# Transposed inverse-Fourier matrices issued during the convolution, and parameter rows loaded from ScalarE's queue into buffers of their own

## The chip, the cores and the metric

The kernel runs on one core of a Trainium2 chip. The metric is the device time of one execution in microseconds (us), from a launch to its end; the profile adds the span from the first to the last instruction. The core has five engines with an instruction stream each: TensorE (PE, matrix products), VectorE (DVE), ScalarE (ACT), GpSimd (POOL) and SyncE (SP). SP, ACT and POOL also issue the DMAs. An engine works through its stream in order, so an instruction that waits holds all that stand behind it on that engine. PE writes its products into banks of PSUM, which ACT or DVE must empty.

## The reference

The kernel computes a block's output and all its gradients, with 2048 tokens, 576 channels, 4608 hidden channels and 128 state pairs per channel:

```
xn = layernorm(x)
K[d,l] = Re( sum_n C[d,n] * exp(dt_d * A[d,n] * l) * dt_d * B[d,n] )
s  = causal convolution of xn with K (by FFT) + xn * Dskip
g  = silu( (silu(xn @ w1) * (xn @ w3)) @ w2 )
out_0 = x + s * g
out_1 ... out_12 = gradients of x, A_re, A_im, B_re, B_im, C_re, C_im, log_dt, Dskip, w1, w3, w2 for grad_out
```

out_2 and out_3 are the gradients of A_re and A_im, out_4 to out_7 those of B and C, out_10 to out_12 those of w1, w3 and w2.

## The kernel before, in words

A scheduler orders the instructions of each engine from planned times (`self.at`), from dependencies and from explicit `issue_after` marks. The stages, with their times in the profiled execution:

- To about 480 us: layer norm, the hidden products and the kernel K, and the forward convolution by matrix products with the Fourier matrices dC and dS (`conv_half`, `dft_block`, L868). The hidden activations are stored to H_dram (L1139).
- `ffn_output` (L1145), to about 690 us: 16 token tiles. For each, SP transposes one tile of H_dram into one of three buffers hcA, hcB, hcC (`begin`, through `nat_transpose`, L1775), and PE multiplies it with w2 (`product`, L1216) into po. SP also stores the tile's results (GS_dram L1237, out_0 L1244) and loads parts of the backward stage (w2T, w2r).
- `backward` (L1614): 18 groups of 256 hidden channels. In each, PE forms ph (L1852) and the weight gradients in pgw (L1893, L1913, L1925); ACT copies them out of PSUM (CAST, L1855, L1897, L1915, L1928); DVE multiplies; SP stores GU and GG (L1875). pgw has two banks. Between the groups stand the backward convolution, in four quarters, and from its end the parameter sums: 36 chunks in two halves, for which SP loads qT (L1775), gz (L1477) and pz (L1480), PE forms et_ps (L1491), and DVE multiplies and sums into S_all (L1496, L1499, through the single buffer pr_q).
- `phase6_inputs`, from about 1435 us: 16 token tiles again. SP transposes GG and GU of a tile into one of two buffers acts (L1775), PE multiplies them with w1 and w3 (px, L1964), DVE adds (gx, L2012), and `ln_bwd_tile` follows: ACT (L2031), POOL (sc, L2039 and L2040), ACT (gxs, L2041), POOL (gxs, L2042), DVE (go, L2071), POOL's store (L2073). ACT loads gxs and go for it (L1953, L1955).

Two pieces are touched by the change. `dft_turn_kernel` fills idC and idS, the matrices of the inverse transform in the backward convolution, by eight transposes of D_dram on SP. The two tiles take the place of dC and dS. Each of the eight is marked to be issued after one of the hc loads of tiles 5 to 12. `phase5_blocks` finishes the parameter gradients in five blocks (four of 2 x 64 rows and one of 2 x 32): twelve loads of rows of B, C and A into X_b on POOL (L1556), the sums ST on DVE (L1561), products with X_b (L1568), a transpose on PE (L1575) that ACT scales back into ST (L1577), products (L1581), eight stores of out_4 to out_7 on POOL (L1587), products (L1591), a copy into X_b on ACT (L1595), and four stores of out_2 and out_3 from it on POOL (L1598). X_b, ST and WO_b share the three buffers of the tag gh6. Each `yield` gives the turn back to the stage around it, which calls the next piece after certain steps of the chunks.

DMAs that SP and ACT issue tell of their landing through eight semaphores, DMAHW0 to DMAHW7, which they take by turns, both engines from the same eight; POOL's DMAs have eight of their own, DMASW0 to DMASW7. In the built program a DMA waits for the semaphore's last DMA where nothing else has made sure of it.

Of the kernel before, what the change touches and what calls it, by code (L numbers as in the profile page):

```python
# [14 lines left out]
BF16 = mybir.dt.bfloat16  # L15
I32 = mybir.dt.int32
I16 = mybir.dt.int16
P = 128
# [82 lines left out]
class K:  # L101
# [745 lines left out]
    def dft_turn_kernel(self):  # L847
        mats = []
        for m, tag in enumerate(("dC", "dS")):
            t = self.matp.tile([P, 4, self.cfg.LS], BF16, name="i" + tag, tag=tag)  # L850
            for i in range(4):
                with self.tc.issue_after(self.hc_loads[5 + 4 * m + i].ins):
                    self.nc.sync.dma_start_transpose(out=t[:, :, i * P:(i + 1) * P], in_=self.D_dram[m, i])
            mats.append(t)
        self.dC, self.dS = mats

# [448 lines left out]
    def params_open(self, S_all, ps):  # L1305
        cfg = self.cfg
        self.sums = ExitStack()
        gkp = self.sums.enter_context(self.pool(name="g_k", bufs=1, side="right"))
        self.qp = self.sums.enter_context(self.pool(name="g_q", bufs=2, side="right"))
        self.zp = self.sums.enter_context(self.pool(name="g_z", bufs=3, side="right"))  # L1310
        self.prp = self.sums.enter_context(self.pool(name="g_pr", bufs=1, side="right"))
        self.S_all, self.ps_T = S_all, ps
        self.gz = []
        for i in range(3):
            z = gkp.tile([P, 2, 2, 2, 8, cfg.LT], BF16, name=f"gz{i}")
            self.nc.vector.memset(z[:], 0.0)
            self.gz.append(z)
        self.half = 0
        self.loaded = {}
# [164 lines left out]
    def param_half(self, ch, dg, gK, qT, pz):  # L1484
# [8 lines left out]
        for x in range(2):  # L1493
# [5 lines left out]
            nc.vector.tensor_reduce(out=self.S_all[:, :, d0:d0 + 4],  # L1499
                                    in_=pr[:].rearrange("p r k (d a) -> p (r k) d a", d=4), op=ALU.add, axis=AX.X)  # L1500

# [39 lines left out]
    def phase5_blocks(self):  # L1541
        nc, cfg, aps = self.nc, self.cfg, self.aps
        D, N = cfg.D, cfg.N
        H = D // 2
        fp = self.fp
        names = ("A_B_re", "A_B_im", "A_C_re", "A_C_im", "A_A_re", "A_A_im")
        tt = nc.vector.tensor_tensor
        for j, c0 in enumerate(range(0, H, 64)):
            R = min(64, H - c0)
            v = slice(0, 2 * R)  # L1550
            if j:
                yield 0
            X = fp.tile([P, 6, N], BF16, name="X_b", tag="gh6")
            for k, name in enumerate(names):
                for h in range(2):
                    nc.gpsimd.dma_start(out=X[R * h:R * h + R, k, :], in_=aps[name][H * h + c0:H * h + c0 + R, :])  # L1556
            yield (c0 + R) // 8
            sv = self.S_all[:].rearrange("p r (c h) -> p r h c", h=2)[:, :, :, c0:c0 + R]
            ST = fp.tile([P, 4, N], FP32, name="ST", tag="gh6")
            sm = ST[:, :, 0:2 * R].rearrange("p k (h c) -> p k h c", h=2)  # L1560
            tt(out=sm[:, 0:2], in0=sv[:, 0:4:2], in1=sv[:, 5:8:2], op=ALU.subtract)  # L1561
            tt(out=sm[:, 2:4], in0=sv[:, 1:4:2], in1=sv[:, 4:8:2], op=ALU.add)
            WO = fp.tile([P, 4, N], FP32, name="WO_b", tag="gh6")
            W = WO[:, 0:2]
            O = WO[:, 2:4].bitcast(BF16).rearrange("p k (two n) -> p (k two) n", two=2)
            Q = self.prp.tile([P, 2, 4, N], FP32, name="pr_q")
            for k in range(2):
                tt(out=Q[v, k, 0:2], in0=X[v, 2 + k:3 + k].to_broadcast([2 * R, 2, N]), in1=X[v, 0:2], op=ALU.mult)  # L1568
            tt(out=W[v, 0], in0=Q[v, 0, 0], in1=Q[v, 1, 1], op=ALU.subtract)
            tt(out=W[v, 1], in0=Q[v, 0, 1], in1=Q[v, 1, 0], op=ALU.add)  # L1570
            yield 0
            pt = self.ps_T.tile([P, 4, N], FP32, name="et_ps")
            with self.tc.issue_after(self.pe_last.ins):
                for k in range(4):
                    nc.tensor.transpose(pt[v, k, :], ST[:, k, 0:2 * R], self.ident_f[:])  # L1575
            for k in range(2):
                nc.scalar.activation(out=ST[v, k:4:2], in_=pt[v, k:4:2], func=ACT.Copy, scale=self.dtb[v, k, j:j + 1])  # L1577
            yield 0
            Q = self.prp.tile([P, 2, 4, N], FP32, name="pr_q")
            for k in range(2):  # L1580
                tt(out=Q[v, k], in0=ST[v, 2 * k:2 * k + 1].to_broadcast([2 * R, 4, N]), in1=X[v, 0:4], op=ALU.mult)  # L1581
            tt(out=O[v, 0:2], in0=Q[v, 0, 0:4:2], in1=Q[v, 1, 1:4:2], op=ALU.subtract)
            nc.vector.scalar_tensor_tensor(out=O[v, 2:4], in0=Q[v, 0, 1:4:2], scalar=-1.0, in1=Q[v, 1, 0:4:2],
                                           op0=ALU.mult, op1=ALU.subtract)
            for k, on in enumerate(("out_6", "out_4", "out_7", "out_5")):
                for h in range(2):
                    nc.gpsimd.dma_start(out=aps[on][H * h + c0:H * h + c0 + R, :], in_=O[R * h:R * h + R, k])  # L1587
            yield 0
            Q = self.prp.tile([P, 2, 4, N], FP32, name="pr_q")
            for k in range(2):  # L1590
                tt(out=Q[v, k, 0:2], in0=W[v, k:k + 1].to_broadcast([2 * R, 2, N]), in1=ST[v, 1:4:2], op=ALU.mult)  # L1591
            tt(out=ST[v, 1], in0=Q[v, 0, 0], in1=Q[v, 1, 1], op=ALU.subtract)
            nc.vector.scalar_tensor_tensor(out=ST[v, 3], in0=Q[v, 0, 1], scalar=-1.0, in1=Q[v, 1, 0],
                                           op0=ALU.mult, op1=ALU.subtract)
            nc.scalar.copy(out=X[v, 0:2], in_=ST[v, 1:4:2])  # L1595
            for k, on in enumerate(("out_2", "out_3")):
                for h in range(2):
                    nc.gpsimd.dma_start(out=aps[on][H * h + c0:H * h + c0 + R, :], in_=X[R * h:R * h + R, k])  # L1598
            acc = self.acc
            for k, (a, b) in enumerate(((ST[v, 1:4:2], X[v, 4:6]), (ST[v, 0:1], W[v, 0:1]), (ST[v, 2:3], W[v, 1:2]))):  # L1600
                nc.vector.tensor_tensor_reduce(out=Q[v, 1, 2:4] if k == 0 else Q[v, 1, 2:3], in0=a, in1=b, scale=1.0, scalar=0.0,
                                               op0=ALU.mult, op1=ALU.add, accum_out=acc[v, k:k + 1])
            tt(out=acc[v, 0:1], in0=acc[v, 0:1], in1=acc[v, 1:2], op=ALU.add)
            tt(out=self.gl[v, j:j + 1], in0=acc[v, 0:1], in1=acc[v, 2:3], op=ALU.subtract)
        yield 0
        pt = self.ps_T.tile([P, 512], FP32, name="et_ps")
        with self.tc.issue_after(self.pe_last.ins):
            nc.tensor.transpose(pt[0:self.NB, 0:P], self.gl, self.ident_f[:])
        gr = fp.tile([self.NB, P], BF16, name="lg_b", tag="gh6")
        nc.scalar.copy(out=gr[:], in_=pt[0:self.NB, 0:P])  # L1610
        for row, vec in self.block_rows(gr, aps["out_8"]):
            nc.gpsimd.dma_start(out=vec, in_=row)
# [567 lines left out]
```

## Time and profile before

| | |
|---|---|
| median of 3 executions | 1776.63 us (1776.33 to 1779.44) |
| the profiled execution | 1770.22 us, span 1768.4 us |
| mean granted clock of PE | 0.983 |
| idle time of PE before its longest waits | 8.33 us at 676, 7.03 us at 717, 5.22 us at 1714 |
| POOL's DMA issues in `phase5_blocks` | about 0.5 us each |
| ACT's DMA issues in the last stage | about 0.34 us each |

In a list of instructions each row has the start and the duration in us, the engine (SPq and ACTq are the queues that issue DMAs), the line, the operation, out<-in with sizes, a count, and in brackets the idle time before it and what ended it. In the table of windows the columns are the stretch, its length, the busy time of PE, PEld, DVE, ACT and POOL with counts, the granted clock of PE, the mean busy share of the DMA engines, and GB/s. The list of DMA issues gives out<-in, queue, count, size and the median time from issue to landing, where known.

### The profile page before, as it was taken

How to read it: one execution, taken by the hardware profiler on the slowest of the kernel's cores; microseconds unless marked ns; L12 is line 12 of the kernel's file. 1: busy time of each engine (PE TensorE's matmuls, PEld its weight loads, DVE VectorE, ACT ScalarE, POOL GpSimd, SP SyncE). 2: the span in 40 equal slices, each digit the busy share in tenths (PEclk: the TensorE clock that was granted, in tenths of full speed). 3: DMA queues.
4: the chain of work that ended last, by engine and by line, in shares of the span. 5: the costliest groups of instructions: out<-in, count | busy, mean ns of one | idle time of the engine just before them, and what ended most of it. 6: DMA issues, size and time to landing. Idle time of an engine off the chain costs nothing. (4 is left out here: it accounts for less than half of the span.)

```text
span 1768.4 us, 34842 instructions
## 1 busy us (share of the span) xinstructions
PE 1632.5 (92%) x13765; PEld 1196.9 (68%) x13765; DVE 1360.9 (77%) x2221; ACT 894.1 (51%) x1509; POOL 328.5 (19%) x530
## 2 busy tenths in 40 slices
PE   6889999999999997799999999999999998999987
PEld 2444444454547775688888888888788776778866
DVE  7658889879784653777978889659899965877765
ACT  4878888886862113565756666554445411110001
POOL 3101111112142110011111101111111233141132
PEclk9999999999999998999999999999999999999999
DMA  7879999978799996768675857589998999999981
GB/s 206 274 252 363 340 352 357 366 251 262 247 279 261 229 219 149 209 183 230 190 193 168 217 171 210 162 233 247 244 244 226 213 260 215 227 242 214 240 172 47
DMA packets 633771, 414.03 MB, mean 234 GB/s; under 512 B 427479, under 2 KB 578247, under 8 KB 628999
## 3 DMA queue, kind: packets, MB, share of 16 engines
q1 hardware_dynamic: 586780, 285.38, 65.2%
q0 software_dynamic: 32704, 114.32, 20.1%
q10 hardware_dynamic: 14122, 12.10, 2.4%
q8 instruction: 108, 1.77, 0.4%
q14 instruction: 57, 0.46, 0.1%
HBM read 130.88 MB, written 191.94 MB: 183 GB/s over the span
## 5 line engine op out<-in xcount | busy, mean ns | idle before, releaser
L1120 PE MATMUL pgu<-wmB_w,xnT 128*128 128x512 bf16 x1152 | 277.1, 379 | 2.5 <-ACT gu_t L1133 2.4
L1964 PEld LDWEIGHTS <-acts 128*128 128x128 bf16 x2304 | 227.9, 100 | 66.1 <-DMA acts<-GU_dram 3.5
L1913 PEld LDWEIGHTS <-xn_bf 128*128 128x128 bf16 x2304 | 224.1, 98 | 42.2 <-issue 16.2
L1496 DVE TENSOR_TENSOR pr_q<-et_ps,pz 128x1024 f32<-128x1024 f32 x144 | 175.9, 1221 | 34.2 <-PE et_ps L1491 25.9
L1964 PE MATMUL px<-wT,acts 128*128 128x288 bf16 x1472 | 193.7, 290 | 0.0
L1120 PEld LDWEIGHTS <-xnT 128*128 128x128 bf16 x1152 | 106.9, 98 | 120.3 <-issue 21.3
L1499 DVE TENSOR_REDUCE S_all<-pr_q 128x32 f32<-128x1024 f32 x144 | 175.2, 1217 | 3.2
L1852 PE MATMUL ph<-w2T,goT 128*128 128x256 bf16 x1440 | 172.8, 274 | 4.6 <-ACT gh L1855 4.6
L1852 PEld LDWEIGHTS <-goT 128*128 128x128 bf16 x1440 | 139.9, 98 | 23.6 <-issue 7.2
L1893 PE MATMUL pgw<-go_o,h_n 128*128 128x288 bf16 x1152 | 148.8, 286 | 0.2
L1133 ACT CAST gu_t<-pgu 128x1024 bf16<-128x1024 f32 x144 | 147.5, 1024 | 0.0
L1913 PE MATMUL pgw<-gu_n,xn_bf 128*128 128x256 bf16 x1152 | 134.5, 272 | 9.2 <-ACT gw L1897 5.3
L1913 PE MATMUL pgw<-gg_n,xn_bf 128*128 128x256 bf16 x1152 | 130.4, 272 | 2.1 <-ACT gw L1915 2.0
L1893 PEld LDWEIGHTS <-h_n 128*128 128x128 bf16 x1152 | 112.1, 98 | 29.5 <-issue 1.8
L1132 ACT ACTIVATE s_t<-pgu 128x512 bf16<-128x512 f32 x144 | 87.9, 610 | 85.2 <-PE pgu L1120 44.3
L1141 POOL DMA_DIRECT2D GUF_dram<-gu_t x72 | 65.3, 908 | 339.2 <-ACT gu_t L1133 312.9
L1915 ACT CAST gw<-pgw 128x256 bf16<-128x256 f32 x144 | 52.2, 373 | 143.2 <-PE pgw L1913 143.2
L1964 PE MATMUL px<-wA,acts 128*128 128x288 bf16 x832 | 113.5, 294 | 5.2 <-DMA acts<-GU_dram 2.9
L1855 ACT CAST gh<-ph 128x512 bf16<-128x512 f32 x144 | 81.6, 601 | 59.1 <-PE ph L1852 57.1
L2031 ACT ACTIVATE go<-gx 128x576 bf16<-128x576 f32 x15 | 10.3, 683 | 186.0 <-DVE gx L2012 179.4
L1136 DVE TENSOR_TENSOR h_t<-s_t,gu_t 128x1024 bf16<-128x1024 bf16 x72 | 49.4, 687 | 47.7 <-ACT gu_t L1133 46.7
L1898 POOL DMA_DIRECT2D out_dram<-gw x36 | 20.2, 560 | 341.7 <-ACT gw L1897 237.7
(329 smaller groups left out, 3016.9 us busy)
## 6 DMA issues: line engine op xcount, KB each, us to landing
GUF_dram<-gu_t POOLq DMA_DIRECT2D x72, 512.0 KB, 5.9
H_dram<-h_t SPq DMA_DIRECT2D x72, 256.0 KB, 5.4
Q_dram<-q_k SPq DMA_DIRECT2D x36, 512.0 KB, 3.9
gg_n<-GUF_dram POOLq DMA_DIRECT2D x18, 1024.0 KB, 6.5
h_n<-GUF_dram POOLq DMA_DIRECT2D x18, 1024.0 KB, 8.8
GG_dram<-gg_n SPq DMA_DIRECT2D x36, 512.0 KB, 10.6
GU_dram<-gu_n SPq DMA_DIRECT2D x36, 512.0 KB, 5.3
E_dram<-E_k SPq DMA_DIRECT2D x54, 256.0 KB, 2.3
```

The lines of the kernel that those rows point to most:

```text
L1120: ins = nc.tensor.matmul(pt, lhsT=xnT[:, c, ts], rhs=wm[w][:, c, :], start=(q == 0 and c == 0), stop=(q == 1 and c == nfull - 1))
L1132: nc.scalar.activation(out=s_t[:, :, q, :], in_=pg.rearrange("p (g f) -> p g f", g=ng), func=ACT.Silu)
L1133: nc.scalar.copy(out=gu_t[:, :, :, q, :], in_=pgu[:].rearrange("p k (g f) -> p k g f", g=ng))
L1141: self.u_stores[step] = nc.gpsimd.dma_start(out=self.GUF_dram[fb * ng:(fb + 1) * ng, :, :, i0:i0 + NT, :].rearrange("g p k t f -> p k g (t ...
L1496: nc.vector.tensor_tensor(out=pr[:].rearrange("p r k e -> p r (k e)"), in0=T[x][:].rearrange("p k z d a -> p (k z d a)")[:, None].to_broad ...
L1499: nc.vector.tensor_reduce(out=self.S_all[:, :, d0:d0 + 4], in_=pr[:].rearrange("p r k (d a) -> p (r k) d a", d=4), op=ALU.add, axis=AX.X)
L1852: self.pe_last = nc.tensor.matmul(ph[j][:, k, :].rearrange("p (a f) -> p a f", f=P), lhsT=lw, rhs=rh, start=(n == 0), stop=(n == nfull))
L1855: self.sc(lambda: nc.scalar.copy(out=gh[:, j], in_=ph[j][:]))
L1893: self.pe_last = nc.tensor.matmul(pgw[pi_][:, 0:pw], lhsT=hn[:, tt, fl * P:(fl + 1) * P], rhs=go_o[:, tt, po:po + pw], start=(tt == 0), st ...
L1913: self.pe_last = nc.tensor.matmul(pw_[:, 0:FG], lhsT=self.xn_bf[:, tt, c * P:(c + 1) * P], rhs=nat[:, tt, :], start=(tt == 0), stop=(tt == ...
L1915: self.sc(lambda: nc.scalar.copy(out=gw[:, c], in_=pw_[:, 0:FG]))
L1964: self.pe_last = nc.tensor.matmul(px[pi_][:, 0:pw], lhsT=acts[i][:, ai, fi, :], rhs=w[:, po:po + pw], start=(n == 0), stop=(n == len(steps ...
```

## The change

The eight transposes of `dft_turn_kernel` lose their marks. In `phase5_blocks` X_b gets a pool of its own with four buffers; block 0's loads are asked for at once and those of block j+1 in two halves within block j; the loads and the stores of out_2 and out_3 are issued by ACT; the first `yield` of each later block goes.

```diff
@@ dft_turn_kernel
             for i in range(4):
-                with self.tc.issue_after(self.hc_loads[5 + 4 * m + i].ins):
-                    self.nc.sync.dma_start_transpose(out=t[:, :, i * P:(i + 1) * P], in_=self.D_dram[m, i])
+                self.nc.sync.dma_start_transpose(out=t[:, :, i * P:(i + 1) * P], in_=self.D_dram[m, i])
@@ params_open
+        self.xbp = self.sums.enter_context(self.pool(name="g_x", bufs=4, side="right"))
@@ phase5_blocks
-        for j, c0 in enumerate(range(0, H, 64)):
+        starts = [*range(0, H, 64)]
+        Xs = []
+
+        def load(j, ks):
+            if j == len(starts):
+                return
+            if j == len(Xs):
+                Xs.append(self.xbp.tile([P, 6, N], BF16, name="X_b"))
+            c0 = starts[j]
+            R = min(64, H - c0)
+            for k in ks:
+                for h in range(2):
+                    nc.scalar.dma_start(out=Xs[j][R * h:R * h + R, k, :], in_=aps[names[k]][H * h + c0:H * h + c0 + R, :])
+
+        load(0, range(6))
+        for j, c0 in enumerate(starts):
             R = min(64, H - c0)
             v = slice(0, 2 * R)
-            if j:
-                yield 0
-            X = fp.tile([P, 6, N], BF16, name="X_b", tag="gh6")
-            for k, name in enumerate(names):
-                for h in range(2):
-                    nc.gpsimd.dma_start(out=X[R * h:R * h + R, k, :], in_=aps[name][H * h + c0:H * h + c0 + R, :])
+            X = Xs[j]
             yield (c0 + R) // 8
...
             tt(out=W[v, 1], in0=Q[v, 0, 1], in1=Q[v, 1, 0], op=ALU.add)
+            load(j + 1, range(0, 3))
             yield 0
...
+            load(j + 1, range(3, 6))
             yield 0
...
             for k, on in enumerate(("out_2", "out_3")):
                 for h in range(2):
-                    nc.gpsimd.dma_start(out=aps[on][H * h + c0:H * h + c0 + R, :], in_=X[R * h:R * h + R, k])
+                    nc.scalar.dma_start(out=aps[on][H * h + c0:H * h + c0 + R, :], in_=X[R * h:R * h + R, k])
```

Lines behind the new code stand 12 later in the changed kernel (L1775 is L1787, L1915 is L1927, L1953 is L1965); the loads of X_b are L1560 there and the stores of out_2 and out_3 L1610.

What stands on SP before, in the output stage at the loads of tiles 12 and 13 (idS is one of the turned matrices, hcA to hcC the hidden activations, GS_dram and out_dram a tile's results):

```order
L853 DMA_TRANSPOSE idS<-D_dram 128x4x128
L1244 DMA out_dram<-o_7652 128x576
L1775 DMA_TRANSPOSE hcA<-H_dram 128x36x128
L1237 DMA GS_dram<-gs_t 128x4x144
L853 DMA_TRANSPOSE idS<-D_dram 128x4x128
L1244 DMA odd_out_109<-o_7758 128x576
L1775 DMA_TRANSPOSE hcB<-H_dram 128x36x128
L1237 DMA GS_dram<-gs_t 128x4x144
```

In the changed kernel no idC or idS stands there. All eight stand on SP at the end of the forward convolution, among the last stores of the kernel's spectrum (KH_dram, KHz_dram) and of the hidden activations (H_dram):

```order
L1001 DMA KH_dram<-k_2_5409 128x2x1152
L1002 DMA KHz_dram<-kz_5410 128x2x576
L1138 DMA H_dram<-h_t 128x2x512 x2
L852 DMA_TRANSPOSE idC<-D_dram 128x4x128 x4
L852 DMA_TRANSPOSE idS<-D_dram 128x4x128 x2
L1001 DMA KH_dram<-k_3_5475 128x2x1152
L1002 DMA KHz_dram<-kz_5476 128x2x576
```

Two more idS follow these rows. On ACT, in the eleventh of the 18 groups (about 1153 to 1167 us in the profile before), stand the copies of the weight gradients from pgw; the semaphores that an instruction waits for are in brackets. Before:

```order
L1915 CAST gw_15030<-pgw 128x256 [waits PE_49]
L1823 ACTIVATE gg_n<-gg_n 128x1024 [waits Activation_49] x2
L1915 CAST gw_15030<-pgw 128x256 [waits PE_49] x2
L1915 CAST gw_15112<-pgw 128x256 [waits DMASW6_49,PE_49]
L1915 CAST gw_15112<-pgw 128x256 [waits PE_49] x3
L1928 CAST gw13t<-pgw 128x256 [waits DMASW1_49,DMASW0_49,PE_49]
```

And in the changed kernel, the same CASTs (L1927 now):

```order
L1927 CAST gw_15033<-pgw 128x256 [waits PE_49] x2
L1560 DMA X_b<-in_A_C_re_dram 64x128 [waits DMAHW5_49]
L1560 DMA X_b<-in_A_C_re_dram 64x128 [waits DMAHW6_49]
L1560 DMA X_b<-in_A_C_im_dram 64x128 [waits DMAHW0_49]
L1560 DMA X_b<-in_A_C_im_dram 64x128 [waits DMAHW2_49]
L1927 CAST gw_15115<-pgw 128x256 [waits DMASW6_49,PE_49]
L1560 DMA X_b<-in_A_A_re_dram 64x128 [waits DMAHW4_49]
L1560 DMA X_b<-in_A_A_re_dram 64x128 [waits DMAHW5_49]
L1560 DMA X_b<-in_A_A_im_dram 64x128 [waits DMAHW6_49]
L1927 CAST gw_15115<-pgw 128x256 [waits PE_49]
L1560 DMA X_b<-in_A_A_im_dram 64x128 [waits DMAHW7_49]
```

The loads of blocks 0 to 3, 48 in all, stand among the CASTs of this group and the next one, each with a wait for a semaphore that SP's DMAs use too. DMAHW0 there was last used by SP's store of GG, DMAHW2 by the first gz load behind it, DMAHW4 by a qT transpose. Before, POOL issued them in the last stage and shortly ahead of it. At the beginning of the last stage ACT has in the changed kernel (go and gxs are the layer-norm inputs of a tile, the loads of X_b those of block 4):

```order
L1967 DMA go_18884<-odd_grad_out 128x576 [waits DMAHW5_49,DMAHW7_49,DMAHW4_49,Pool_49]
L1607 CAST X_b<-ST 128x256 [waits DVE_49,Activation_49]
L1610 DMA out_dram<-X_b 64x128 [waits DMAHW0_49,Activation_49]
L1610 DMA out_dram<-X_b 64x128 [waits DMAHW1_49]
L1610 DMA out_dram<-X_b 64x128 [waits DMAHW2_49]
L1610 DMA out_dram<-X_b 64x128 [waits DMAHW3_49]
L1965 DMA gxs_18876<-GXN_dram 128x576 [waits DMAHW5_49,DMASW3_49,DMASW2_49]
L1965 DMA gxs_18882<-GXN_dram 128x576 [waits DMAHW6_49,DMASW0_49]
L1560 DMA X_b<-in_A_B_re_dram 32x128 [waits DMAHW2_49,DMAHW3_49,DMAHW1_49,DMAHW7_49,DMAHW0_49,DVE_49]
```

Before, the gxs loads stood right behind the CAST into X_b there. DMAHW0 to DMAHW3 were last used by SP's four transposes into acts.

## Prediction

> **What bounds the kernel now.** I read the page's busy shares first, then the table of TensorE's waits in the two stretches that the change touches, then the lists of instructions around each wait.
>
> ```profile
> PE 1632.5 (92%) x13765; PEld 1196.9 (68%) x13765; DVE 1360.9 (77%) x2221; ACT 894.1 (51%) x1509; POOL 328.5 (19%) x530
> PE po L1216 <- DMA hcC<-H_dram: 8.3, 1, 8.3
> PE et_ps L1491 <- DVE pr_q L1496: 9.8, 6, 5.2
> ```
>
> TensorE (PE) is busy 92% of the span, so the time is its work plus the places where it stands still. The second line is its worst wait for the hidden activations in the forward output stage (us in total, times, longest); the third its wait for VectorE (DVE) in the last stage, 5.2 us of it at one place. So I count stalls of PE that go, and look for those that come. A stall costs more than its length:
>
> ```profile
> 640.00 4.08 PE L1216 MATMUL po<-w2a,hcC 128*128 128x288 bf16 x32
> 676.46 6.42 PE L1216 MATMUL po<-w2a,hcC 128*128 128x288 bf16 x32 [8.33 <-DMA hcC<-H_dram]
> 1492.54 0.38 PE L1491 MATMUL et_ps<-gz,qT 128*128 128x128 bf16 x4 [2.20 <-DVE pr_q L1496]
> 1490.00:1500.00 10.00, 7.80 (x58) 5.78 (x58) 9.49 (x8) 0.00 (x0) 0.00 (x0) 0.83 1.21 235
> ```
>
> The same 32 matmuls take 4.08 us undisturbed and 6.42 us after the wait of 8.33: 2.3 us more. After a wait of only 2.20 us the granted clock of that 10 us stretch (third number from the end) is 0.83, some 1.7 us lost. I price a stall above 2 us at its length plus 1.7, and a long one at plus 2.3. The Trainium skill ("TensorE: Matmul & The Clock Gate", Part 1, on HAM oscillation) wants idle gaps above about 3.4 us before the clock falls; this trace shows it after 2.20, so the measurement decides. By the page each short stall below would cost 1.7 us less.
>
> **First part, the matrices turned earlier.** SyncE (SP) now issues eight small transposes (idC, idS) between the loads of the hidden activations:
>
> ```profile
> 636.56 3.60 PE L1216 MATMUL po<-w2g,hcB 128*128 128x288 bf16 x28
> 643.95 1.20 SPq L853 DMA_TRANSPOSE idS<-D_dram  x1
> 645.87 7.87 SPq L1775 DMA_TRANSPOSE hcB<-H_dram  x1
> 662.38 8.03 SPq L1775 DMA_TRANSPOSE hcC<-H_dram  x1
> ```
>
> The hcB load at 645.87 could start when PE has read the old hcB, at 636.56 + 3.60 = 640.2; SP comes to it 5.7 us late, behind the transposes. Without them hcB, and with it the hcC load of 662.38 that PE waits for, move up by 5.7: the stall falls from 8.33 to 2.6, its slow clock from 2.3 to 1.7. That is -6.3 us. Bounds: 0, if hcC lands no sooner because the DMA engines and not SP hold it (a rival), and -10.6, if the stall goes whole. In the convolution the eight now stand among these stores:
>
> ```profile
> 484.31 0.42 SPq L1003 DMA_DIRECT2D KHz_dram<-kz  x1
> 488.45 5.52 SPq L1139 DMA_DIRECT2D H_dram<-h_t  x2
> SPq L1775 <- PE po L1216: 25.7, 9, 5.8
> ```
>
> SP issues nothing from 484.7 to 488.45, and between 560 and 680 its loads waited 25.7 us in nine places for PE to free a buffer (third line): some microseconds are to spare, so 0, at most +1.5 if the H_dram stores behind them come late.
>
> **Second part, the parameter rows.** What goes is GpSimd's (POOL's) traffic in front of the layer-norm step:
>
> ```profile
> 1696.89 2.13 POOL L1598 DMA_DIRECT2D out_dram<-X_b  x4 [8.67 <-ACT X_b L1595]
> 1707.04 0.50 POOL L1556 DMA_DIRECT2D X_b<-in_A_A_re_dram  x1 [2.47 <-DMA X_b<-in_A_B_re_dram]
> 1712.04 0.82 DVE L2071 SCALAR_TENSOR_TENSOR go<-gx,rstd,gxs 128x576 bf16<-128x576 f32 x1 [11.77 <-POOL gxs L2042]
> 1714.04 0.58 PE L1491 MATMUL et_ps<-gz,qT 128*128 128x128 bf16 x4 [5.22 <-DVE pr_q L1496]
> 1574.65 0.38 PE L1491 MATMUL et_ps<-gz,qT 128*128 128x128 bf16 x4 [0.98 <-DVE pr_q L1496]
> ```
>
> From 1696.89 POOL issues four stores and twelve loads and waits for some to land; the gxs product behind them holds DVE 11.77 us and PE 5.22. With both on ScalarE (ACT), the stall at 1714 goes with its slow clock, and that at 1574.65, of the same kind: -5.2 - 2.3 - 1.0 = -8.5 us.
>
> What comes in is on ACT's queue. The order of the changed kernel puts all 48 loads of blocks 0 to 3 far ahead, among the CASTs that empty the PSUM banks of pgw, and each waits for a DMA semaphore; there are eight for SP's and ACT's DMAs together, so a new DMA waits for the landing of the one that used its semaphore before. This trace has such a wait:
>
> ```profile
> 1518.92 7.76 SPq L1775 DMA_TRANSPOSE acts<-GG_dram  x1
> acts<-GG_dram SPq DMA_TRANSPOSE x1, 10.3
> 1525.63 0.87 ACT L2041 ACTIVATE gxs<-xn_bf,sc 128x576 f32<-128x576 bf16 x1 [1.51 <-POOL sc L2039]
> 1529.27 0.34 ACTq L1953 DMA_DIRECT2D gxs<-GXN_dram  x1
> ```
>
> ACT is free at 1526.5, yet issues its load only at 1529.27, when SP's transpose lands (1518.92 + 10.3 = 1529.2; the second line is the list of DMA issues, with the median time to landing last). ACT stands still meanwhile, and what is queued behind waits with it. The first place where that meets CASTs:
>
> ```profile
> 1157.80 6.93 PE L1913 MATMUL pgw<-gg_n,xn_bf 128*128 128x256 bf16 x62
> 1159.21 2.77 SPq L1477 DMA_DIRECT2D gz<-gK_dram  x2
> 1162.71 2.34 SPq L1775 DMA_TRANSPOSE qT<-Q_dram  x1
> gz<-gK_dram SPq DMA_DIRECT2D x4, 64.0 KB, 5.4
> 1159.53 0.37 ACT L1915 CAST gw<-pgw 128x256 bf16<-128x256 f32 x1 [1.72 <-PE pgw L1913]
> 1161.28 0.37 ACT L1915 CAST gw<-pgw 128x256 bf16<-128x256 f32 x1 [1.38 <-PE pgw L1913]
> ```
>
> PE runs without a pause there, and each CAST comes the moment PE has filled a bank (ACT idles 1.38 us between them; two banks, so a CAST may be 1.4 us late). In the new order the CAST of 1159.53 stands behind a load that waits for the first gz load, 1159.21 + 5.4 = 1164.6; with the issue of 0.34 it starts at 1165.0, 5.4 late, and PE stalls 4.0. The next CAST, now due at 1165.3, stands behind a load that waits for qT; with the 5.4 us of gz for it, 1168.1 and 0.4 of issue, 3.2 late, a stall of 1.8. With one slow clock: +7.5 us. The second place:
>
> ```profile
> 1187.57 1.37 SPq L1875 DMA_DIRECT2D GU_dram<-gu_n  x2
> 1189.04 5.37 SPq L1875 DMA_DIRECT2D GG_dram<-gg_n  x2
> GU_dram<-gu_n SPq DMA_DIRECT2D x2, 512.0 KB, 7.5
> 1194.86 0.37 ACT L1915 CAST gw<-pgw 128x256 bf16<-128x256 f32 x1 [1.38 <-PE pgw L1913]
> 1240.21 0.38 PE L1491 MATMUL et_ps<-gz,qT 128*128 128x128 bf16 x4 [3.07 <-DMA gz<-gK_dram]
> ```
>
> Block 3's loads wait for these stores: the first GG store lands, by GU's 7.5, at 1196.5, which makes the CAST of 1194.86 2.0 late and the stall 0.6. But the stores themselves now share the eight semaphores with ACT's loads, and the GU store waits for a qT transpose; PE is by then about 2 us later than before and SP some 6. Then the CAST is 6 late, the stall 4.6 to 5.1. I take 5.1 + 1.7 = +6.8, the lower end being +0.6, because the order has both waits. SP's lateness also lengthens the wait of 3.07 at 1240: +1 (0 to 2). Together +15.3 us, with ends of 0 (no load holds a CAST) and about +21 (each landing 1 us longer, four waits in a row, one more slow clock): ACT's 48 issues themselves, 48 x 0.34 = 16 us, lie in its idle time.
>
> The third place is the last stage. Block 0's four out stores now stand on ACT, each with a semaphore of SP's acts transposes (10.3 us to landing), and ahead of the gxs loads and block 4's loads; SP's next acts load shares a semaphore with one of these:
>
> ```profile
> 1466.06 5.38 SPq L1775 DMA_TRANSPOSE acts<-GG_dram  x1
> 1475.73 0.79 PE L1964 MATMUL px<-wA,acts 128*128 128x288 bf16 x5 [2.35 <-DMA acts<-GG_dram]
> 1448.68 0.43 DVE L1568 TENSOR_TENSOR pr_q<-X_b 128x256 f32<-128x256 bf16 x1 [3.09 <-DMA X_b<-in_A_C_re_dram]
> 1478.20 0.82 DVE L2071 SCALAR_TENSOR_TENSOR go<-gx,rstd,gxs 128x576 bf16<-128x576 f32 x1 [6.71 <-POOL gxs L2042]
> ```
>
> PE already waits 2.35 us for that load; if SP is 5 us later, +4.8 and 0.6 of clock. On the other side DVE no longer waits for X_b (3.09) nor as long for POOL (6.71), so the 2.20 at 1492 goes with its clock (-3.9). I take +1.5, ends -4 and +9. That block 1's ST step on DVE and its transposes on PE stand earlier, since X_b holds no buffer of theirs, moves the same work within idle time of DVE: 0.
>
> **Sum.** -6.3 + 15.3 + 1.5 - 8.5 = +2.0 us. The profiled execution took 1770.22 (span 1768.4 and 1.8 around it), the median of three runs is 1776.63; added to the median: 1778.6. Two runs of this kernel can be told apart from about 0.2%, here 3.6 us.
>
> **Rivals.** (1) *SP and ACT hold each other in the last stage.* Block 4's loads wait for block 0's stores, these for SP's transposes, and SP's acts load at 1466 for block 4. Then the third place costs its upper end, +9 in place of +1.5: 1786. It decides when block 4's first load is issued after 1466. For it: 10.3 us to landing for each transpose. Against: only one chain, and the loads of blocks 1 and 2 have left that stretch, so landings should be shorter. (2) *ACT is not held.* Then +15.3 falls to 0 and the third place to 0: -14.8, 1761.8; half of it gives 1769. For it: ACT is busy 51% and a load is 0.34 us. Against: the row at 1529.27. The Trainium skill ("DMA: Bandwidth & Descriptors", section "Issuing engines are not separate DMA queues") says that a DMA started from another engine saves only the time to initiate it, and names no wait between issuers; by it this rival would hold. (3) *The first part does nothing*, because hcC took 676.46 - 662.38 = 14.1 us to land and the DMA engines, not SP, are its limit: +6.3, 1784.9.
>
> **Chances.** The forecast's own case 0.46, between 1774 and 1783: two thirds of it within 0.2% of 1776.63 (0.31), one third above (0.15). Rival 1 0.16 and rival 3 0.08, both slower. Rival 2 0.30, of which 0.24 is faster and 0.06, a partial relief, no change. So faster 0.24, no change 0.37, slower 0.39. The range 1766 to 1789 takes in half of rival 2, rivals 1 and 3 and the ends of the terms taken together.
>
> **What would show it.** In the changed profile the wait for hcC should be near 2.6 us, and idC and idS issued near 481 to 490. ACT should show loads L1560 between 1138 and 1205 with idle time ahead of them, and PE new waits at pgw for ACT's CAST, two or three of 1.5 to 5 us. The waits at 1574 and 1714 should be gone. The forecast is wrong if PE has no wait at pgw above 1 us (rival 2), if the wait for hcC is still 8 us (rival 3), or if PE waits over 7 us for acts near 1480 (rival 1).

## The result, and the profile after

| | before | after |
|---|---|---|
| median of 20 executions on the same chip | 1768.57 us (1752.48 to 1779.44) | 1784.61 us (1765.21 to 1811.61) |
| ratio, 95% interval | | 1.0078 [1.0049, 1.0107] |
| profiled execution | 1770.22 us, clock 0.983 | 1805.05 us, clock 0.980 |

The change makes the kernel slower by 0.78%, some 14 us (9 to 19). The forecast was +2.0. The ratios here and below are of undisturbed executions alone, and the profiled execution of the changed kernel is a disturbed one, 20 us above its median, so it shows where waits stand, and the sizes are taken from the runs of the parts below.

The page's busy shares and the table of PE's waits, after (us in total, times, longest):

```profile
PE 1636.9 (91%) x13708; PEld 1200.7 (67%) x13765; DVE 1361.4 (75%) x2221; ACT 894.8 (50%) x1509; POOL 288.7 (16%) x450
PE et_ps L1491 <- DMA gz<-gK_dram: 16.7, 7, 6.3
PE pgw L1925 <- ACT gw L1927: 14.9, 18, 5.2
PE pgw L1925 <- ACT gw L1909: 11.5, 11, 4.3
PE po L1215 <- DMA hcA<-H_dram: 6.0, 1, 6.0
PE po L1215 <- DMA w2g<-in_B_w_dram: 3.7, 3, 1.7
PE po L1215 <- DMA hcC<-H_dram: 1.2, 1, 1.2
```

PE's work is nearly the same; it stands still more. The wait for hcC has fallen from 8.3 to 1.2, where 2.6 was forecast. But the wait for hcA has grown from 0.9 to 6.0, three waits for w2g are new, and the waits at pgw for ACT and at et_ps for gz have become the largest of the backward stage.

**The first part's places.** In the list of SP's instructions at the end of the convolution the transposes stand where the order had put them:

```profile
481.25 5.34 SPq L852 DMA_TRANSPOSE idC<-D_dram  x4
486.69 2.52 SPq L852 DMA_TRANSPOSE idS<-D_dram  x2
...
491.00 7.92 SPq L852 DMA_TRANSPOSE idS<-D_dram  x2
499.01 4.28 SPq L1138 DMA_DIRECT2D H_dram<-h_t  x3
...
558.01 13.97 SPq L1787 DMA_TRANSPOSE hcA<-H_dram  x1
...
670.04 10.12 SPq L1787 DMA_TRANSPOSE hcC<-H_dram  x1
```

They take SP 5.34 + 2.52 + 7.92 = 15.8 us, one of them 6.0 alone. Three H_dram stores that began at 488.45 before begin at 499.01, and the load of hcA at 558.01 where it stood at 550.63. DVE and PE then wait (the lists of their instructions, with the idle time ahead in brackets):

```profile
507.48 0.69 DVE L1135 TENSOR_TENSOR h_t<-s_t,gu_t 128x1024 bf16<-128x1024 bf16 x1 [3.44 <-DMA H_dram<-h_t]
```

```profile
521.84 2.30 PE L902 MATMUL et_ps<-V,cT 128*128 128x288 bf16 x16 [2.27 <-DVE V L926]
578.59 6.03 PE L1215 MATMUL po<-w2a,hcA 128*128 128x288 bf16 x32 [6.00 <-DMA hcA<-H_dram]
684.50 4.09 PE L1215 MATMUL po<-w2a,hcC 128*128 128x288 bf16 x32 [1.24 <-DMA hcC<-H_dram]
```

A chain: the late store holds h_t's buffer, DVE waits 3.44 for it, V comes late and PE waits 2.27; the loads of w2g and hcA come late too. At 578.59 the clock loss is there as well: the 32 matmuls take 6.03 where the undisturbed 32 take 4.08. The hcC load that PE waited for before goes out at 670.04, 7.7 us later than in the kernel before (662.38), not sooner. The wait for it is short because PE, held further up, comes to it only at 683.3, where it came at 668.1 before.

**The second part's places.** ACT, SP and PE in the eleventh group:

```profile
1164.70 1.26 ACTq L1560 DMA_DIRECT2D X_b<-in_A_C_re_dram  x1
1171.62 1.12 ACTq L1560 DMA_DIRECT2D X_b<-in_A_C_im_dram  x2
1172.83 0.37 ACT L1927 CAST gw<-pgw 128x256 bf16<-128x256 f32 x1 [8.21 <-DMA gz<-gK_dram]
```

```profile
1166.42 2.53 SPq L1477 DMA_DIRECT2D gz<-gK_dram  x2
```

```profile
1173.26 2.08 PE L1925 MATMUL pgw<-gg_n,xn_bf 128*128 128x256 bf16 x9 [5.20 <-ACT gw L1927]
```

This is the wait that the prediction took from the order. From about 1166.0 to 1171.62 ACT issues nothing; its next load goes out 5.2 us after SP's gz load (5.4 from issue to landing before). The CAST behind it has waited 8.21 us, ended by the landing of gz, a transfer that it does not use. PE stands 5.20.

In the last stage, a wait of the kind that should have gone:

```profile
1744.38 3.08 ACTq L1610 DMA_DIRECT2D out_dram<-X_b  x4
1747.52 0.68 ACT L2043 ACTIVATE go<-gx 128x576 bf16<-128x576 f32 x1 [3.16 <-issue]
```

```profile
1752.97 0.38 PE L1491 MATMUL et_ps<-gz,qT 128*128 128x128 bf16 x4 [4.90 <-DVE pr_q L1496]
```

POOL no longer holds the layer-norm step with its DMAs here; ACT does, 3.16 us with the four stores that moved to it. DVE stands 7.88 us in all before its go at 1750.97, and PE behind it.

### The profile page after: what moved, and what is told of

It is laid out like the page before. It is cut to its first block, busy times and chain, and to the rows that moved or that the text cites. A ratio compares the mean times of both kernels' runs of the same rounds, so it can differ in the third digit from the quotient of the medians.

```text
span 1803.3 us, 34738 instructions
## 1 busy us (share of the span) xinstructions
PE 1636.9 (91%) x13708; PEld 1200.7 (67%) x13765; DVE 1361.4 (75%) x2221; ACT 894.8 (50%) x1509; POOL 288.7 (16%) x450
## 3 DMA queue, kind: packets, MB, share of 16 engines
q0 software_dynamic: 30144, 113.14, 19.5%
## 5 line engine op out<-in xcount | busy, mean ns | idle before, releaser
L1119 PE MATMUL pgu<-wmB_w,xnT 128*128 128x512 bf16 x1101 | 269.5, 379 | 5.6 <-ACT gu_t L1132 2.4
L1925 PEld LDWEIGHTS <-xn_bf 128*128 128x128 bf16 x2304 | 227.8, 99 | 62.0 <-issue 32.3
L1925 PE MATMUL pgw<-gu_n,xn_bf 128*128 128x256 bf16 x1152 | 138.3, 277 | 15.3 <-ACT gw L1909 11.5
L1925 PE MATMUL pgw<-gg_n,xn_bf 128*128 128x256 bf16 x1152 | 134.7, 277 | 11.8 <-ACT gw L1927 11.5
L1927 ACT CAST gw<-pgw 128x256 bf16<-128x256 f32 x144 | 52.5, 374 | 161.5 <-PE pgw L1925 134.5
L1882 DVE TENSOR_TENSOR gu_n<-gh,gu_n 128x1024 bf16<-128x1024 bf16 x72 | 49.1, 684 | 46.7 <-ACT gh L1867 46.6
```

What stands on the lines that cost most here:

```text
L1119: ins = nc.tensor.matmul(pt, lhsT=xnT[:, c, ts], rhs=wm[w][:, c, :], start=(q == 0 and c == 0), stop=(q == 1 and c == nfull - 1))
L1925: self.pe_last = nc.tensor.matmul(pw_[:, 0:FG], lhsT=self.xn_bf[:, tt, c * P:(c + 1) * P], rhs=nat[:, tt, :], start=(tt == 0), stop=(tt == ...
L1927: self.sc(lambda: nc.scalar.copy(out=gw[:, c], in_=pw_[:, 0:FG]))
```

## The experiments

Twelve kernels, each with twelve executions (e4 and e8 six), against executions of the kernel before on the same chip. "Ratio" is this kernel to the kernel before. To see where a run's time lies, I take the start of the same DVE instruction in its profile and in that of before, and what their distance grew by in three stretches: the end of the convolution and the output stage (461 to 735 us of before), the groups with the parameter sums (1147 to 1400), the last stage (1400 to 1765).

| run | ratio, 95% interval | 461-735 | 1147-1400 | 1400-1765 |
|---|---|---|---|---|
| changed kernel | 1.0078 [1.0049, 1.0107] | +6.5 | +37.8 | -6.4 |
| e1, transposes early only | 1.0057 [1.0027, 1.0087] | +4.0 | -4.1 | -0.1 |
| e2, rows on ACT only | 1.0071 [1.0042, 1.0099] | -6.6 | +22.6 | -5.0 |
| e3, transposes at tiles 2 to 9 | 1.0028 [0.9996, 1.0059] | +3.8 | -4.1 | -7.1 |
| e4, rows held on ACT | 1.0100 [1.0054, 1.0146] | +1.1 | -4.1 | +9.3 |
| e5, no transposes | 0.9955 [0.9926, 0.9983] | -7.0 | -1.2 | -6.5 |
| e6, rows on POOL | 0.9961 [0.9934, 0.9988] | -3.7 | -0.5 | -8.9 |
| e7, loads on ACT, stores on POOL | 1.0060 [1.0030, 1.0091] | -2.3 | +19.5 | -15.4 |
| e8, half as many loads on ACT | 1.0140 [1.0092, 1.0188] | +0.7 | +24.4 | -8.2 |
| e9, transposes behind the last load | 1.0019 [0.9989, 1.0050] | +5.9 | -4.1 | -8.6 |
| e10, e9 with e6 | 0.9981 [0.9945, 1.0016] | +0.6 | -3.4 | -12.9 |
| e11, e10 with the rows held | 1.0024 [0.9992, 1.0055] | +5.6 | -4.1 | +1.3 |
| e12, transposes in SP's gaps, with e6 | 0.9949 [0.9919, 0.9978] | -4.7 | -3.5 | -14.0 |

How much one profile can tell is in the table itself. In the first stretch e2, e4, e6, e7 and e8 have the code of before, and lie from -6.6 to +1.1. In the last, e1, e3, e5 and e9 have it, and lie from -8.6 to -0.1. So the one profile on which the prediction rests was a late one in these stretches: the mean of such runs, with before itself as 0, is -1.8 in the first stretch, -2.7 in the groups (e1, e3, e5, e9) and -4.5 in the last.

**e1 and e2: each part alone.** e1 takes the marks from the transposes and leaves the rest as before; e2 is the change with the marks put back:

```diff
-                with self.tc.issue_after(self.hc_loads[5 + 4 * m + i].ins):
-                    self.nc.sync.dma_start_transpose(out=t[:, :, i * P:(i + 1) * P], in_=self.D_dram[m, i])
+                self.nc.sync.dma_start_transpose(out=t[:, :, i * P:(i + 1) * P], in_=self.D_dram[m, i])
```

> Only the first part of the change: the eight transposes of D_dram lose their marks; the parameter rows stay as before. Theory (both parts cost): in the changed kernel's profile the eight transposes hold the stores of KH, KHz and H_dram and the w2g and first hc loads behind them on SP, and PE is about 16 us late at the first hcA wait (6.0 us) and gets about 10 back at the last hcC wait; so +4 to +8 us against before, with the waits for w2g and for hcA there again, and the wait for hcC below 2 us. Rival (the loss early in the output stage is a disturbance of that one profiled run, the first part gains as forecast): -4 to -8 us, no wait for hcA above 2 us.

> Only the second part: X_b in four buffers of its own, its loads and the stores of out_2 and out_3 issued by ACT; the transposes keep their marks. Theory (both parts cost): the loads hold ACT's copies out of PSUM at the pgw banks, and what comes late behind them (stores, gg loads, gz) adds further stalls up to the last stage; +5 to +12 us against before, with two or more waits of PE for ACT's CAST of 2 us and more between 1150 and 1260. Rival (the second part gains, all of the loss is the first part's): -5 us or less, no such wait.

Both cost: 0.57% (10 us) and 0.71% (13 us). Their sum, 1.28% with an interval of about 0.4 either way, is above the 0.78% of both together; the intervals overlap, so whether they share something is open. e1's PE shows the wait for hcA of the changed kernel again, and none above 0.3 us for hcC:

```profile
578.72 3.53 PE L1215 MATMUL po<-w2a,hcA 128*128 128x288 bf16 x16 [8.36 <-DMA hcA<-H_dram]
```

e2's ACT and PE:

```profile
1161.55 0.37 ACT L1928 CAST gw<-pgw 128x256 bf16<-128x256 f32 x1 [8.68 <-DMA gz<-gK_dram]
1165.48 0.37 ACT L1928 CAST gw<-pgw 128x256 bf16<-128x256 f32 x1 [3.56 <-DMA X_b<-in_A_A_re_dram]
1168.90 1.25 ACTq L1561 DMA_DIRECT2D X_b<-in_A_C_re_dram  x2
...
1204.22 2.98 ACTq L1561 DMA_DIRECT2D X_b<-in_A_A_re_dram  x2
1208.76 0.37 ACT L1928 CAST gw<-pgw 128x256 bf16<-128x256 f32 x1 [5.56 <-DMA X_b<-in_A_A_re_dram]
```

```profile
1161.97 3.57 PE L1926 MATMUL pgw<-gg_n,xn_bf 128*128 128x256 bf16 x16 [5.67 <-ACT gw L1928]
1174.51 1.47 PE L1865 MATMUL ph<-w2T,goT 128*128 128x256 bf16 x12 [2.76 <-ACT gh L1868]
1209.18 3.57 PE L1926 MATMUL pgw<-gg_n,xn_bf 128*128 128x256 bf16 x16 [4.03 <-ACT gw L1928]
1257.06 0.59 PE L1492 MATMUL et_ps<-gz,qT 128*128 128x128 bf16 x4 [4.22 <-DMA gz<-gK_dram]
1491.54 4.73 PE L1977 MATMUL px<-wA,acts 128*128 128x288 bf16 x26 [5.32 <-DMA acts<-GG_dram]
1508.11 3.99 PE L1977 MATMUL px<-wA,acts 128*128 128x288 bf16 x18 [5.31 <-DMA acts<-GU_dram]
```

So the rivals of both (an early loss by chance, a gain of the second part) fall. The second ACT row is one that the prediction had not priced: a CAST that stands behind ACT's own loads. The last two rows show it at the second place. Between 1199.41 and 1208.72 ACT issues seven loads, 0.5 to 1.6 us each and 7.9 us in all. Its one longer pause, 1.1 us, ends at 1206.7, when the first GG store lands (issued at 1199.81, 6.9 us to landing).

**e3: the transposes at tiles 2 to 9.**

```diff
-                with self.tc.issue_after(self.hc_loads[5 + 4 * m + i].ins):
+                with self.tc.issue_after(self.hc_loads[2 + 4 * m + i].ins):
```

> The kernel before, with the eight transposes marked behind the hidden-activation loads of tiles 2 to 9 instead of 5 to 12: not in the convolution, and none left at tiles 10 to 12. Theory (the place among the convolution's stores is what costs, and the last transposes of before are what delays the hcC load of tile 14): the gain forecast for the first part without its loss, -4 to -9 us, the wait for hcC below 3 us. Rival (SP has no time for them at tiles 2 to 4 either): the wait for hcA or hcB grows by what hcC loses, 0 to +4 us.

```profile
687.61 2.82 PE L1216 MATMUL po<-w2a,hcC 128*128 128x288 bf16 x11 [8.33 <-DMA hcC<-H_dram]
```

My theory fell: no gain (0.28%, interval from -0.04 to 0.59), and the wait for hcC is 8.33 although no transpose stands near it, so it is not tied to the transposes of tiles 10 to 12. Whether SP has time to spare at tiles 2 to 4 is not shown: the wait for hcA is 4.24 here, and 0.4 to 3.9 in the six profiles with the old code of this stretch.

**e4: the loads held on ACT.** As e2, with

```diff
-                    nc.scalar.dma_start(out=Xs[j][R * h:R * h + R, k, :], ...)
+                    with self.tc.issue_after(self.last["sc"].ins):
+                        nc.scalar.dma_start(out=Xs[j][R * h:R * h + R, k, :], ...)
```

> The second part alone, with each load of X_b queued on ACT behind the last ACT instruction of the groups that was there when it was asked for, so that all stand in the last group and the last stage; own buffers, ACT's queue and all else as in the second part. Theory (what costs is that the loads ran far ahead among the CASTs of two groups): no new waits at pgw between 1150 and 1380, the waits of the last stage at POOL's traffic partly gone: -2 to -9 us against before, and at least 8 us below the run with the second part alone. Rival (the loads cost on ACT's queue wherever they stand, by its issues or by waits for SP's transposes in the last stage): within 3 us of the second part alone.

```profile
1425.68 0.70 ACT L1911 CAST gw<-pgw 128x288 bf16<-128x288 f32 x2 [17.73 <-DMA X_b<-in_A_A_im_dram]
```

```profile
1426.13 7.52 PE L1927 MATMUL pgw<-gu_n,xn_bf 128*128 128x256 bf16 x48 [9.09 <-ACT gw L1911]
```

The groups are clear (-4.1), but the same thing happens in the last group: ACT works through 17 loads for 17.73 us, and the copies behind them hold PE 9.09. The theory that running ahead was the harm fell; the loads cost at both places on ACT that were tried.

**e5: no transposes at all.** `dft_turn_kernel` does nothing, so the values of this kernel are others and only its time is used.

> The kernel before with the eight transposes of D_dram left out altogether (the backward convolution uses the untransposed matrices, so its values and what follows from them are others; the work on PE is the same). It bounds what any other place for them can gain. Theory (the long wait for a hidden-activation load in the output stage falls on one or another tile from run to run, whether or not a transpose stands ahead of it, because DMA and not SP holds those loads): -3 to +2 us against before, and a wait of 3 us or more for hcA, hcB or hcC is still there. Rival (as forecast, SP's time in the transposes holds the loads): -6 us or more, no wait for an hc load above 3 us.

```profile
570.89 4.50 PE L1209 MATMUL po<-w2a,hcA 128*128 128x288 bf16 x18 [5.41 <-DMA hcA<-H_dram]
661.85 8.37 SPq L1768 DMA_TRANSPOSE hcC<-H_dram  x1
703.70 0.42 SPq L1294 DMA_DIRECT2D cCSb<-CS_dram  x1
710.72 0.30 PE L875 MATMUL et_ps<-gs,cCSb 128*128 128x144 bf16 x2 [3.20 <-DMA cCSb<-CS_dram]
```

-0.45%, 8 us (3 to 13). Neither expectation holds whole. A long wait for an hc load is there without any transpose (5.41 for hcA), and the hcC load goes out at 661.85, only 0.5 us sooner than before (662.38). Nor are the 8 us all the transposes'. The wait for cCSb is 3.20 here, 7.03 before and 6.5 to 7.4 in every other run, wherever the transposes stand. Here alone SP's order has the cCSb load ahead of eight loads of a and az (at 703.70; before it stood behind them, at 713.06). That is up to 3.8 of the 8 us; an order with this load ahead and the transposes kept was not tried. So the transposes themselves cost less than the 8 us measured where they stood. Moving them into the convolution costs e1's 10 us on top of that.

**e6: the rows on POOL.** As e2, with `nc.gpsimd` for `nc.scalar` at the loads and at the stores of out_2 and out_3.

> The second part with POOL's queue in place of ACT's for the loads of X_b and the stores of out_2 and out_3; own buffers and the loads a block ahead as in the second part, and the loads free to run ahead in POOL's order. Theory (ACT's DMAs wait for semaphores that SP's long transfers hold, and ACT's copies stand behind them; POOL's DMAs have semaphores of their own): no wait at pgw for ACT's CAST above 1 us between 1150 and 1260, waits for acts as short as before (2.4 us), 10 us or more below the run with the second part alone, so 0 to -5 us against before. Rival (it is the loads' place among the groups, or their traffic, that costs, on whatever queue): within 4 us of the second part alone, with waits at pgw or ph of 2 us and more in the same groups.

```profile
1159.49 0.37 ACT L1928 CAST gw<-pgw 128x256 bf16<-128x256 f32 x1 [1.37 <-PE pgw L1926]
```

```profile
1183.91 7.07 PE L1926 MATMUL pgw<-gu_n,xn_bf 128*128 128x256 bf16 x48 [3.23 <-ACT gw L1910]
```

ACT idles 1.4 us between the CASTs again, as before. One wait of 3.23 is left, more than the 1 us expected: ACT had to wait for a gg load that POOL issues among those of X_b. Same buffers, same look-ahead, another queue: 0.9961 instead of 1.0071, 1.1% apart. That is the clearest answer of the study: it was ACT's queue that cost. The Trainium skill ("DMA: Bandwidth & Descriptors", section "Issuing engines are not separate DMA queues") says that starting DMAs on several engines at once saves only the time to initiate them. It names a saving and no cost; here the choice of the engine moved the time by 19 us.

**e7: loads on ACT, stores on POOL.** As e2, with `nc.gpsimd` for `nc.scalar` at the stores alone.

> The second part with only the loads of X_b on ACT; the stores of out_2 and out_3 go back to POOL. Theory (the two waits of some 5 us for acts in the last stage come from these stores, which stand on ACT behind SP's transposes and share their semaphores): both waits for acts at 2.5 us or below, the waits at pgw of the second part still there, so 4 to 8 us below the second part alone. Rival (the acts waits come from SP's lateness after the groups, not from the stores): the waits for acts stay at 4 us and more, and the time stays within 3 us of the second part alone.

```profile
1488.20 3.36 PE L1977 MATMUL px<-wA,acts 128*128 128x288 bf16 x26 [2.38 <-DMA acts<-GG_dram]
```

The profile does what the theory says (2.38 for acts, and 10 us less in the last stage than e2), the times do not: 1.0060 against 1.0071, with intervals of 0.3%. And in e10, with the stores on POOL as well, the wait for acts is 7.12. So what the stores cost on ACT stays open; most of the loss is the loads'. e7 and e6 show that best: they ran on the same chip and differ in the queue of the loads alone, with medians of 1776.12 and 1757.85 us.

**e8: half as many loads.** One DMA for both halves of a parameter's rows:

```diff
-                for h in range(2):
-                    nc.scalar.dma_start(out=Xs[j][R * h:R * h + R, k, :], in_=aps[names[k]][H * h + c0:H * h + c0 + R, :])
+                nc.scalar.dma_start(out=Xs[j][0:2 * R, k, :], in_=aps[names[k]].rearrange("(h r) n -> h r n", h=2)[:, c0:c0 + R, :])
```

> The second part with one load for both halves of a parameter's rows in place of two: 6 in place of 12 a block, with the same bytes, on ACT as before. Theory (each load costs only where its semaphore was last used by one of SP's long transfers, and eight loads in a row use all eight): the first wait at pgw, for the gz load, stays at 4 us or more; fewer rounds of the eight, so 0 to 4 us below the second part alone. Rival (the loads cost by their number, about 0.5 us of ACT each): half of what the second part costs, so some 6 us below the second part alone, and no wait at pgw above 3 us.

```profile
1184.63 1.07 ACTq L1560 DMA_DIRECT2D X_b<-in_A_C_re_dram  x1
...
1192.71 6.15 ACTq L1560 DMA_DIRECT2D X_b<-in_A_C_im_dram  x1
```

```profile
1199.88 2.72 PE L1864 MATMUL ph<-w2T,goT 128*128 128x256 bf16 x12 [9.81 <-ACT gh L1867]
```

Both expectations fell; it is slower still, 1.0140. A load of twice the bytes takes ACT's queue 1.07 us where two of e2 take 1.25, so little is saved by the number. All 24 loads now stand in one group instead of two, one of them takes 6.15 us to issue, and PE stands 9.81 us behind them. Why the whole is dearer than in e2 was not tried further.

**e9: the transposes behind the last hidden-activation load.**

```diff
-                with self.tc.issue_after(self.hc_loads[5 + 4 * m + i].ins):
+                with self.tc.issue_after(self.hc_loads[15].ins):
```

> The kernel before with all eight transposes marked behind the last hidden-activation load (tile 15), where SP has nothing to load for some 20 us. Theory (what the transposes cost is SP's time ahead of loads that PE waits for, and the more the earlier; behind the last load nothing waits for SP until the backward convolution): the gain of leaving them out, -5 to -9 us against before, and the first product with idC or idS on PE no later than before by more than 1 us. Rival (the eight cost wherever they stand, by their DMA traffic or by the stores of GS behind them, which the backward convolution loads): 0 +- 3 us, with the wait for cCSb or gs at the start of the backward convolution 4 us longer.

```profile
682.40 8.98 SPq L853 DMA_TRANSPOSE idC<-D_dram  x4
691.43 6.79 SPq L853 DMA_TRANSPOSE idS<-D_dram  x4
698.32 0.53 SPq L1237 DMA_DIRECT2D GS_dram<-gs_t  x1
```

```profile
700.74 0.76 DVE L1236 TENSOR_TENSOR gs_t<-go_t,g 128x576 bf16<-128x576 bf16 x1 [9.81 <-DMA GS_dram<-gs_t]
```

```profile
703.57 0.86 PE L1277 MATMUL ptr<-ident_bf,go_o 128*128 128x128 bf16 x5 [6.37 <-DVE go_o L1234]
```

No gain (0.19%, interval from -0.11 to 0.50). The rival had the time right, and the store of GS: the eight take 15.8 us in a row, the store stands behind them, DVE waits 9.81 for its buffer and PE 6.37 for DVE. The wait for cCSb, where the rival looked, is no longer than before (6.67). It is the chain of the convolution again, with other names.

**e10 and e11: e9 with the rows on POOL, free and held.** e10 is e9 with e6; e11 holds the loads behind `self.last["gp"]`.

> Both parts in the places that the runs so far favour: the transposes behind the last hidden-activation load, X_b in buffers of its own with loads and stores on POOL. Theory (the two parts touch stretches far apart and add up): the sum of the two alone, -12 to -17 us against before. Rival (they share what they gain, or the waits of the last stage take it back): no better than the better of the two alone, -5 to -8 us.

> As the run before it, with the loads of X_b queued behind the last of POOL's DMAs of the groups that was there when they were asked for, so that they stand in the last group and the last stage. Theory (running ahead on POOL costs little: one wait of some 3 us for a copy at 1184): 0 to -4 us against the run before it. Rival (held loads stand on POOL ahead of the layer-norm step's products again, as before the change, and the wait near 1714 comes back): +3 to +8 us against the run before it.

e10 gives -0.19% (interval from -0.55 to 0.16), the rival's side, as e9 gives nothing to add. e11 is 7 us above e10 on the same chip (1766.02 to 1758.78), but their intervals against before overlap: that running ahead is better on POOL is likely, not shown. In e11 DVE stands 8.38 us for POOL's gxs at 1485, the wait that the change wanted to remove, at another tile; in e10 it is 2.94 there.

**e12: the transposes in SP's gaps, the rows on POOL.** Four behind the out_0 store of tile 13, four behind that of tile 14:

```diff
-                with self.tc.issue_after(self.hc_loads[5 + 4 * m + i].ins):
+                with self.tc.issue_after(self.o_stores[13 + m].ins):
```

> As the run with the transposes behind the last hidden-activation load and the rows on POOL, with the eight transposes split: four behind the out_0 store of tile 13, four behind that of tile 14, where SP stood idle for some 9 to 10 us each, so that no store of GS stands behind all eight. Theory (what spoilt the place behind the last load was the GS store that stood behind 15.8 us of transposes, for which DVE and then PE waited): no wait of PE for go_o at its last transposes above 2 us, the start of the backward group earlier by 5 to 8 us than with the eight in one block, and -8 to -14 us against before. Rival (whatever is gained there is lost to the wait for cCSb behind it, or to waits elsewhere that differ from run to run): 0 to -6 us, as with the rows on POOL alone.

```profile
682.79 6.65 SPq L853 DMA_TRANSPOSE idC<-D_dram  x4
689.54 0.53 SPq L1238 DMA_DIRECT2D GS_dram<-gs_t  x1
...
691.67 5.53 SPq L853 DMA_TRANSPOSE idS<-D_dram  x4
```

1751.26 us against 1762.12 of before on that chip, 0.9949 [0.9919, 0.9978], 9 us (4 to 14): a version faster than both kernels. PE's wait for go_o has fallen from 6.4 in e9 to 1.0, and the first stretch is 5.3 us shorter than in e10 (-4.7 to +0.6), as the theory expected. Its interval overlaps those of e10 and of e6, so that the place of the transposes adds to e6 is shown in the profile's waits, not in the times.

## Why the prediction was wrong in size and where

**First part, forecast -6.3, measured +10 (5 to 15).** Two steps failed. The first is "some microseconds are to spare, so 0, at most +1.5". I priced the place in the convolution by one idle stretch on SP (484.7 to 488.45, under 4 us) and put eight transposes into it at no cost, though their own rows stood in the trace: 1.2 to 2.7 us each, 13.0 in all. They took 15.8. What is queued behind them on SP was named in the text, H_dram's stores, but not what waits for those: the buffer h_t on DVE, then w2g and hcA on PE.

The second is "Without them hcB, and with it the hcC load of 662.38 that PE waits for, move up by 5.7". Without any transpose (e5) SP is not late for hcB at all: PE has read the old hcB at 647.98, and the load goes out at 648.02. But PE itself is 7.8 us later there than before (640.2), for it has waited 5.41 for hcA at 570.89, and so the hcC load goes out only 0.5 us sooner, at 661.85. It takes 13.1 us to land, where it took 14.0. Freeing SP thus moved the wait from one tile to another instead of removing it. That is nearer to rival 3, in which SP is not what holds these loads; what sets their pace was not found. That the wait for hcC came out below the forecast (1.24 for 2.6, 0.3 in e1) is luck: PE came later, the load did not come sooner. The base, too, was one execution: in five other profiles of the same code that wait is 8.16, 6.08, 5.61, 3.79 and none. What the transposes could give back at most is e5's 8 us, less what the earlier cCSb load gives there, and only to a place where nothing waits.

**Second part, what comes in: forecast +15.3, in the profile of e2 +22.6, and +25 against the mean of the runs without it.** The mechanism was right at the first place. A CAST waits there for the landing of gz in e2 (8.68), in e7 (8.10) and in the changed kernel (8.21), and on POOL (e6) that wait is absent; the stall is 5.67 for 4.0. The 1.8 at the next CAST did not come (0.36), but 2.76 at ph did. At the second place the size fits, 4.03 for 5.1, and the reason mostly does not: 7.9 us of ACT's time are the loads' own issue, and 1.1 the wait for the GG store. So the step that failed is "ACT's 48 issues themselves, 48 x 0.34 = 16 us, lie in its idle time", a term put at nothing. In e2 the 48 took 33.5 us, 0.5 to 1.6 each, and CASTs stood behind them; in e4, too, 17 loads fill the 17.73 us. On top came 1.66 more at pgw, at 1235, and 4.22 for gz, where I had 1 us beyond 3.07; and the 3.07 of the kernel before is itself absent in e1, e3 and e9.

**What goes: forecast -8.5.** The stall near 1714 is there in e1 too (4.96 at 1713), but not in e3, e5 and e9, where nothing was done about it; it is gone in e2, and in the changed kernel one of 4.90 stands at 1752.97. Against the runs with the old code, e2's last stage gains 0.5 us. The kernels with the loads ahead and the stores on POOL lie lower there (e6, e7, e10 and e12 from -8.9 to -15.4, the old code from -8.6 to 0), so some of the gain may be real when the stores do not move to ACT. Two stalls of one execution could not give its size.

**The third place and the rivals.** Rival 1 wanted a wait for acts above 7 us; it is 5.32 and 5.31 in e2, 2.4 in all in the changed kernel, and 7.12 in e10, where no store stands on ACT: it can happen, and what decides was not found. Rival 2, ACT not held, is refuted. Rival 3 was right that the output stage gains nothing; that the first part takes time in the convolution was in none of the three.

**The chances.** Slower had the most, 0.39, but for rivals 1 and 3 and a third of the forecast's own case; what came, the loss of the first part in the convolution, had none of it.

**The base.** The forecast was added to a median of three, 1776.63; twenty executions on that chip have 1768.57, others 1762 to 1767. A part of what looked like a small miss (1784.61 against 1778.6) is that: the change itself cost seven times the forecast 2 us. That the measured time lies in the stated range, 1766 to 1789, is in part luck: the base was 8 us too high, and the first part has the wrong sign.

## What to carry to other kernels

A DMA put on a compute engine's queue is also a wait: in this toolchain it may stand for another engine's transfer, and every instruction behind it stands too, so look up which semaphores it shares before choosing the queue, count its issue as time of that engine, and prefer one whose own work can be late (POOL here). Before pricing a wait for a load as its queue's lateness, look at what the queue did in that time. Before moving DMAs into a "gap", add up all of them by their own rows and follow the first thing queued behind them to the buffer that it frees. A stall of one profile is a sample: where several versions have the same code, compare them before pricing its removal.

## What was not expected of the hardware

- A transpose of 128x512 takes 1.2 to 2.7 us on SP's queue where they stand apart in the kernel before, 13.0 us for the eight. Eight behind each other took 15.8 us in the changed kernel and in e9, 11.6 in e10 and 11.5 in e11; as two fours in e12 12.2. One alone took 6.0 in the changed kernel.
- A load of gxs took ACT's queue 0.34 us in the last stage before; a 16 KB load of X_b took some 0.6 in a row of them, and up to 1.6 at the second place of e2.
- The wait for one load of 128x36x128 (hcC) lies between 0 and 8.3 us in six profiles with the same instructions up to there, and the executions of the kernel before spread over 1749 to 1781 us on the chips used.
